# A tau-thresholded attention with a gated FFN on one core: plain float32 scores on halves of the rows in place of split ones, k kept for two chunks, 70 crossbar tiles and a new order

## The chip, the cores and the metric

The kernel runs on one core of one Trainium2 chip. The metric is the device time in microseconds; the kernel before takes 888.61 us, the median of three runs (888.23 to 890.14). One further run was profiled.

## What is computed

Eight batches of 576 tokens pass through an attention with eight heads of 64 channels and then through an FFN with a gate made by a three-tap convolution over the tokens:

```
scores = scale * q @ k.T                       # 576 x 576 per batch and head, float32
thresh = max(scores, axis=-1) - tau
scores = where(scores >= thresh, scores, -1e9)
attn = softmax(scores)                         # with 1e-9 added to the sum
x = concat over heads of attn @ v              # 576 x 512 per batch
h = relu(x @ w_in)                             # 512 -> 1024
conv = sum over 3 taps of conv_w[k] * shifted h
out = (h * sigmoid(conv)) @ w_out              # 1024 -> 512
```

## The kernel before

**Tiling.** Heads are taken in pairs, four pairs to a batch. The tokens of a batch are 4 full tiles of 128 rows and one of 64; tiles 0 and 1 are one chunk, tiles 2, 3 and 4 the next, so there are 16 chunks, 64 pairs of heads in chunks, and 160 units (one tile of one pair of heads). A full tile has two heads of scores, each 128 x 576 in two PSUM banks of 288 columns; the small tile has both heads in one buffer. That makes 288 score buffers in all, held in two PSUM buffers (`ps_s`).

**A unit** (`unit`, L573). TensorE makes the scores, VectorE takes the row maximum (L612), ScalarE the exponential (L619), VectorE masks it and sums (L622), and GpSimd (or ScalarE, L658) scales the result `em` by the reciprocal of the sum (L660).

**Turning `em`.** The product with v needs `em` with keys on the partitions, in the buffer `eT`. Most tiles are turned on TensorE: nine 128 x 128 transposes to a full tile (`transposes`, L719), gathered four at a time in a PSUM buffer `ps_t` and moved out by ScalarE (L714). The others go over the DMA crossbar (`cross`, L675): `em` is copied as two planes of 16-bit halves into `parts`, one plane by ScalarE (L337) and one by GpSimd (L339), `parts` is written to DRAM as `rows` (L692), and two transposing DMAs read it back into `eT` (L697). The table `CROSS` says how many full tiles of a chunk and pair go that way: 42 in all, none in batch 0.

**Product and FFN.** `attend` (L762) multiplies `eT` by v: first `mixed` (L774), 64-row matmuls on 64-column quarters of the array, then L783, 128 rows by 64 columns. The FFN (`mm1`, L799, and `mm2`, L854) uses the whole array with values rounded to fp32r and their remainders, three matmuls to a product. The FFN of a chunk is spread over the units of the chunk after it.

**Scores before.** In batch 0, and for every small tile, a score is a plain float32 product (L597): the 64 channels lie twice on the 128 partitions, the first half of the array makes keys 0 to 287 and the second half keys 288 to 575 at the same time. For the full tiles of batches 1 to 7 `split` is set (L604): q and k are each cut into a part rounded to fp32r and the remainder, these are stacked on the 128 partitions, and a head takes four fp32r matmuls of the whole array. `prep_k` (L532) and `prep_q` (L546) make these parts: two activations and a subtraction for k (L537, L538, L344), one activation and a subtraction for q (L552, L344), and DMAs that copy the parts to the other half of the partitions (L526, L560).

**The order.** Nothing runs in the order in which it is written. Every step is recorded with an engine, a duration, a rank and what it reads and writes; `Plan.run` then plays them through with a clock of its own and emits the instructions in the order that results. The rank is lowered by the entry of `AHEAD` for the kind of step. TensorE's steps have a kind: `full` (whole array), `turn` (transpose), `rows` and `cols` (parts of the array). The table `SWITCH` holds what a change of kind costs in this clock, and `KEEP` how much rank it may give up to avoid one. Each engine then executes its own list in order and waits on semaphores.

Of the kernel before, what the change touches and what calls it, by code (L numbers as in the profile page):

```python
# [22 lines left out]
AHEAD = {'mask': -0.546, 'norm': 0.0, 'parts': 0.747, 'gate': 0.0, 'evac': 0.244, 'low': 0.0, 's': 8.8, 's4': 7.75, 't': 2.623, 'a': 4.072, 'prep': 5.282, 'w': 2.013, 'load': 10.996}  # L23

LATENCY = {'pe': 159.52, 'act': 151.014, 'dve': 99.075, 'pool': 67.058, 'ring': 1611.881}

HOLD = {'pool': 162.449, 'dve': 91.329}
# [3 lines left out]
NEAR = 16  # L31
# [3 lines left out]
MOE = (2, 2)  # L35
BACKLOG = {'pool': 6860.0, 'dve': 120.0, 'act': 9000000000.0}
WRATE = (1.704, 1.59)
# [18 lines left out]
CROSS = ((1, 0, 1, 0), (1, 1, 1, 1))  # L56
LATE = {'load': 663.0, 'copy': 382.0, 'rows': 456.0, 'turn': 383.0}

KEEP = {'rows': 3.209, 'cols': 1.6, 'turn': 3.226, 'full': 1.708}
# [18 lines left out]


class Later:  # L80


    def __init__(self, view, n):
        self.view, self.shape = view, (n,)

    def __getitem__(self, key):
        return self.view()[key]
# [169 lines left out]
def tile_tau_attention_gated_ffn(  # L257
# [3 lines left out]
    qt: bass.AP,  # L261
    kt: bass.AP,
# [102 lines left out]
    def split(src, n, name, high, low, hr, lr, queue="sp"):  # L365
# [3 lines left out]
        stage = plan.buf(wk, "ks", 4, [P, 2, S], U32, name)  # L369
        value = plan.buf(wk, "xq", 2, [P, 2, 2 * P], U32, f"{name}_f")  # L370

        def flat():
            return stage[:].rearrange("p a b -> p (a b)")[:, :2 * n]
# [5 lines left out]
        def v(dtype=F32):  # L379
            return value[:].rearrange("p a b -> p (a b)")[:, :n].bitcast(dtype)  # L380
# [51 lines left out]
    QW = 2 * P  # L432
# [62 lines left out]
    def plain(b):  # L495
        return b == 0

    def prep_rows(i, b, p, o, w, tag):

        k = plan.buf(wk, "xk", 2, [P, S + D], F32, f"k_{i}")  # L500
        q = plan.buf(wk, tag, 2, [P, 2, w], F32, f"{tag}_{i}")
        a = AHEAD["prep"]

        if i:
            put(S + D, lambda: nc.sync.dma_start(k[:], kp[b, p]), w=[(k, 0), (k, 1)], ahead=a + 2)
# [6 lines left out]
        if w < P:  # L512
            op("act", act(2 * w), lambda: nc.scalar.activation(q[:], q[:], AF.Copy, scale=0.125), w=[(q, 0), (q, 1)], ahead=a)
            return k, q
        for j in range(2):
            op("act", act(w), lambda j=j: nc.scalar.activation(q[:, j], q[:, j], AF.Copy, scale=0.125), w=[(q, j)], ahead=a)
        return k, q

    def halves(dst, src, of, ahead):

# [384 lines left out]
    def prep(i, j):  # L905
        if i >= len(pairs):
            return
# [124 lines left out]
```

## Time and profile before

| | |
|---|---|
| median of three runs | 888.61 us (888.23 to 890.14) |
| profiled execution | 891.74 us |
| its span, first to last instruction | 889.9 us |
| granted TensorE clock, mean | 0.998 |

The span is 1.8 us shorter than the profiled execution's own time, and that execution is 3.1 us longer than the median. In the profile PE is TensorE's matmuls and PEld its weight loads, DVE is VectorE, ACT ScalarE, POOL GpSimd and SP the queue that issues most DMAs. A float32 matmul stands in the profile as two matmul instructions, each of which streams all columns; an fp32r one stands as one. In a timeline row the first number is the start and the second the length until the last of the merged instructions has ended; since matmuls are pipelined, the time that one takes from the next is read from start to start.

### The profile page before, as it was taken

The numbers are of one execution on the slowest core, as the hardware profiler recorded it, in microseconds if no ns is written. First come the engines' busy times: TensorE is split into PE (matmuls) and PEld (weight loads), VectorE is DVE, ScalarE is ACT, GpSimd is POOL, SyncE is SP. The second block draws the span as 40 slices with busy tenths as digits, with TensorE's granted clock in tenths as the row PEclk, the third lists the DMA queues.
The fourth block names the chain that finished last, engine by engine and source line by source line (L and its number), as shares of the span: only waits on it lengthen the run. The fifth ranks groups of instructions, "written<-read, shape, count | busy, mean of one in ns | idle before, by whom it ended". The sixth has DMA issues, their size and how long they took to land.

```text
span 889.9 us, 18227 instructions
## 1 busy us (share of the span) xinstructions
PE 861.2 (97%) x5930; PEld 691.7 (78%) x5930; DVE 748.0 (84%) x1902; ACT 712.5 (80%) x1489; POOL 476.8 (54%) x617
## 2 busy tenths in 40 slices
PE   4899999999999999999999999999999999999998
PEld 2445778778778788878888788897888888887896
DVE  5999999988989689987979689996998879997542
ACT  5989898888878787888877788887877888885642
POOL 3465865646646555565645556564663655553322
PEclk9999999999999999999999999999999999999999
DMA  7554366588855777659754697548955578454200
GB/s 235 177 166 140 92 178 163 142 223 205 222 147 136 207 187 202 144 157 239 194 170 115 155 238 197 141 118 242 225 150 131 156 219 211 117 150 106 66 24 36
DMA packets 176702, 145.22 MB, mean 163 GB/s; under 512 B 115552, under 2 KB 146528, under 8 KB 176608
## 3 DMA queue, kind: packets, MB, share of 16 engines
q1 hardware_dynamic: 175744, 142.15, 60.3%
q10 hardware_dynamic: 864, 1.90, 0.6%
q8 instruction: 48, 0.79, 0.4%
q14 instruction: 46, 0.38, 0.1%
HBM read 50.62 MB, written 34.21 MB: 95 GB/s over the span
## 4 chain that ended last, share of the span: by engine, by line
PE 80%; ACT 9%; DVE 6%; DMA 3%; issue 2%; SPq 0%; POOL 0%; ACTq 0%; DVEq 0%
PE po L863 20%; PE ph L812 19%; PE ps_s L604 13%; PE pa L783 12%; PE ps_t L719 9%; PE ps_s L597 4%; DVE em L622 2%; ACT eT L714 2%; ACT em L619 2%; PE pa L774 2%; DVE few L612 2%; DMA xk<-in_kt_dram 1%; PE pw_stage L418 1%; DMA k<-in_kp_dram 1%; DMA ks<-xk 1%
## 5 line engine op out<-in xcount | busy, mean ns | idle before, releaser
L660 POOL TENSOR_SCALAR em<-em,few 128x576 f32<-128x576 f32 x231 | 190.7, 832 | 185.9 <-DVE few L646 151.3
L612 DVE TENSOR_REDUCE few<-ps_s 128x1 f32<-128x576 f32 x288 | 210.7, 748 | 37.4 <-PE ps_s L597 20.0
L619 ACT ACTIVATE em<-ps_s,few 128x576 f32<-128x576 f32 x288 | 206.1, 739 | 43.0 <-DVE few L612 40.4
L812 PE MATMUL ph<-x,w1h 128*128 128x322 f32 (+1 forms) x1024 | 238.4, 304 | 0.5 <-ACT hp L821 0.5
L622 DVE SCALAR_TENSOR_TENSOR em<-ps_s,few,em 128x576 f32<-128x576 f32 x288 | 225.3, 811 | 14.6 <-ACT em L619 8.5
L344 POOL TENSOR_TENSOR gl<-t,gh 128x255 fp32r<-128x255 f32 (+9 forms) x192 | 123.4, 652 | 163.7 <-ACT gh L842 157.8
L812 PEld LDWEIGHTS ph<-x,w1h 128*128 128x128 f32 x1024 | 174.0, 189 | 2.1 <-issue 1.1
L714 ACT ACTIVATE eT<-ps_t 128x512 f32<-128x512 f32 (+2 forms) x332 | 149.1, 474 | 10.6 <-PE ps_t L719 8.4
L604 PE MATMUL ps_s<-ks,qs 128*128 128x288 f32 x896 | 151.9, 304 | 2.6 <-DVE em L622 0.6
L812 PE MATMUL ph<-x,w1l 128*128 128x322 f32 (+1 forms) x512 | 151.2, 295 | 0.0
L604 PEld LDWEIGHTS ps_s<-ks,qs 128*128 128x128 f32 x896 | 127.5, 188 | 27.5 <-issue 19.7
L719 PE MATMUL ps_t<-ident,em 128*128 128x128 f32 x934 | 137.0, 277 | 5.1 <-ACT eT L714 3.3
L783 PE MATMUL pa<-eT,v 128*64 128x320 f32 (+1 forms) x1024 | 132.8, 410 | 0.0
L719 PEld LDWEIGHTS ps_t<-ident,em 128*128 128x128 f32 x934 | 109.1, 142 | 27.5 <-issue 8.0
L863 PE MATMUL po<-w2h,gh 128*128 128x512 f32 x288 | 117.5, 408 | 0.0
L783 PEld LDWEIGHTS pa<-eT,v 128*64 128x64 f32 x1024 | 70.1, 137 | 58.2 <-issue 15.4
L863 PE MATMUL po<-w2l,gh 128*128 128x512 f32 x288 | 112.9, 392 | 0.0
L863 PE MATMUL po<-w2h,gl 128*128 128x512 f32 x288 | 112.9, 392 | 0.0
L827 DVE SCALAR_TENSOR_TENSOR t<-hp,cr 128x321 f32<-128x321 f32 (+1 forms) x128 | 82.4, 645 | 22.7 <-ACT hp L821 21.3
L812 PEld LDWEIGHTS ph<-x,w1l 128*128 128x128 f32 x512 | 96.7, 189 | 0.3
L832 DVE SCALAR_TENSOR_TENSOR t<-t,hp 128x321 f32<-128x321 f32 (+1 forms) x128 | 76.7, 600 | 12.6 <-ACT t L834 12.0
L827 DVE SCALAR_TENSOR_TENSOR t<-hp,cr,t 128x321 f32<-128x321 f32 (+1 forms) x128 | 85.7, 672 | 0.5
(78 smaller groups left out, 1079.1 us busy)
## 6 DMA issues: line engine op xcount, KB each, us to landing
rows<-parts SPq DMA_DIRECT2D x42, 576.0 KB, 3.4
qs<-qs SPq DMA_DIRECT2D x168, 128.0 KB, 2.9
k<-in_kp_dram SPq DMA_DIRECT2D x35, 320.0 KB, 3.4
v<-in_vc_dram SPq DMA_DIRECT2D x36, 288.0 KB, 4.2
out_dram<-ot SPq DMA_DIRECT2D x36, 256.0 KB, 2.6
xk<-in_kt_dram SPq DMA_DIRECT2D x28, 288.0 KB, 3.7
ks<-xk SPq DMA_DIRECT2D x56, 144.0 KB, 3.6
xq<-in_qt_dram SPq DMA_DIRECT2D x56, 128.0 KB, 3.0
```

The source lines that it names most:

```text
L344: engines[e].tensor_tensor(dst, x, y, op=ALU.subtract)
L604: nc.tensor.matmul(ps[:, c, :CH], lhsT=q[:, i, h, o:o + n], rhs=k[:, h, c * CH:(c + 1) * CH], start=(i == 0), stop=(i == 1))
L612: nc.vector.tensor_reduce(few[:rows, nm], ps[:rows, :, :CH], op=ALU.max, axis=mybir.AxisListType.XY, negate=True)
L619: nc.scalar.activation(view(), ps[:rows, :, :CH], AF.Exp, bias=few[:rows, nm])
L622: nc.vector.scalar_tensor_tensor(view(), ps[:rows, :, :CH], few[:rows, th], view(), op0=ALU.is_ge, op1=ALU.mult, accum_out=few[:rows, total])
L660: engines[e].tensor_scalar(sl, sl, LEAST, few[:rows, 10 + h:11 + h], op0=ALU.add, op1=ALU.mult)
L714: "act", act(w, True), lambda dst=dst, src=src: nc.scalar.activation(dst(), src(pt), AF.Copy),
L719: nc.tensor.transpose(out=pt[:, at:at + P], in_=em[:, int(b * P):int(b * P) + P], identity=ident[:])
L783: nc.tensor.matmul(pa[j * D:(j + 1) * D, :w], lhsT=vt[:, blk, :], rhs=eT[:, :w // D, blk, :], start=False, stop=(r == 3))
L812: nc.tensor.matmul(ph[:, :an], lhsT=w1[w][:, cb, fs], rhs=xs[cb][:, h, :an], start=(cb == 0 and i == 0), stop=(cb == NCB - 1 and i == 2))
L827: nc.vector.scalar_tensor_tensor(t[:, :kn], hp[:, o + k:o + kn + k], cr[:, j, f:f + 1], y, op0=ALU.mult, op1=ALU.add)
L863: nc.tensor.matmul(po[:], lhsT=x[:, f, at:at + P], rhs=w[:, f, :], start=(f == 0 and i == 0), stop=(f == NFB - 1 and i == 2))
```

## The change

All scores become plain float32 products on halves of the rows, as batch 0 had them. `split`, `prep_k`, `prep_q` and `halves` go, with the inputs `qt` and `kt` in which q and k lay once. For every pair of heads `prep` now loads q doubled over the partitions, and k doubled in the first chunk of a batch; k stays in its buffer for the second chunk (`KEEPK`, six buffers). The factor 0.125 is applied to k once (`eighth`), where batch 0 applied it to q in each chunk. `CROSS` sends 70 full tiles over the crossbar instead of 42: one tile of every pair in the even chunks, and two or one in the odd ones. The weights get staging buffers of their own. The numbers that steer `Plan.run` are replaced (`AHEAD`, `LATENCY`, `HOLD`, `KEEP`, `LATE`, `MOE`, `NEAR`, `WRATE`); of these a few lines are shown, since what they do is seen in the order only.

```diff
-NEAR = 16
+NEAR = 8
...
-MOE = (2, 2)
+MOE = (2, 3)
...
-WRATE = (1.704, 1.59)
+WRATE = (1.767, 1.972)
...
-CROSS = ((1, 0, 1, 0), (1, 1, 1, 1))
+KEEPK = 1
+XKB = 6
+CROSS = ((1, 1, 1, 1), (2, 1, 2, 1))
...
+        k = whole[i - NP][0] if o and KEEPK else plan.buf(wk, "xk", XKB, [P, S + D], F32, f"k_{i}")
+        q = plan.buf(wk, "q", QB, [P, 2, w], F32, f"q_{i}")
...
+                def eighth(e, x=x):
+                    copy(e, x(), x(), 0.125)
+
+                op("act", act(n), eighth, w=parts, ahead=a, other=[("pool", pool1(n)), ("dve", 65 + n * 0.53)] if i else [], port=True)
...
-                for c in range(2):
-                    for i in range(2):
+                for r, j in enumerate(js):
+                    for c in range(2):
+                        on = slice(c * D, (c + 1) * D)
+                        at = j * CH + r * D
                         nc.tensor.matmul(
-                            ps[:, c, :CH], lhsT=q[:, i, h, o:o + n], rhs=k[:, h, c * CH:(c + 1) * CH], start=(i == 0), stop=(i == 1)
+                            ps[r * n:(r + 1) * n, c, :CH], lhsT=q[on, j, o:o + n], rhs=k[on, at:at + CH],
+                            start=True, stop=True
                         )
...
-                "pe", 534 if split else 490, mm, w=[(ps, 0)],
+                "pe", 490, mm, w=[(ps, 0)],
```

What this does to the lists of the engines: on PE the 224 groups of split scores (four matmuls each) become 224 groups of plain ones, and 322 groups of transposes become 238 (934 transposes become 682). The rows here and in the prediction name tiles as the program does: `ps_s` scores, `pa` the product with v, `ph` and `po` the first and second product of the FFN, `ps_t` transposes.

The first place is PE in batch 3, at the scores of pair 1 in the first chunk (`ps_s_0` and `ps_s_1` are the two heads of a tile; the chunk has two tiles). Before:

```order
L604 MATMUL ps_s_0_3991<-ks_1_3743,qs_3804 128x288 x4
L774 MATMUL pa_4000<-eT_3762,v_2822 64x320 x2
L774 MATMUL pa_4003<-eT_3855,v_2862 64x320 x2
L604 MATMUL ps_s_1_4013<-ks_1_3743,qs_3804 128x288 x4
L783 MATMUL pa_4000<-eT_3762,v_2822 64x320 x8
L783 MATMUL pa_4003<-eT_3855,v_2862 64x320 x8
L604 MATMUL ps_s_0_4071<-ks_1_3743,qs_3804 128x288 x4
L604 MATMUL ps_s_1_4079<-ks_1_3743,qs_3804 128x288 x4
L812 MATMUL ph_4_4088<-x_3055,w1h 128x256
```

and now:

```order
L549 MATMUL ps_s_0_3598<-k_2302,q_3445 128x288 x2
L549 MATMUL ps_s_1_3606<-k_2302,q_3445 128x288 x2
L720 MATMUL pa_3613<-eT_3361,v_2615 64x320 x2
L720 MATMUL pa_3616<-eT_3454,v_2623 64x320 x2
L729 MATMUL pa_3613<-eT_3361,v_2615 64x320 x8
L729 MATMUL pa_3616<-eT_3454,v_2623 64x320 x8
L549 MATMUL ps_s_0_3662<-k_2302,q_3445 128x288 x2
L549 MATMUL ps_s_1_3670<-k_2302,q_3445 128x288 x2
L665 MATMUL ps_t_0_3674<-ident,em_3543 128x128 x4
L758 MATMUL ph_5_3682<-x_2698,w1h 128x256
```

The two heads of a tile now stand together and beside the products with v, where one head stood between two of these products before.

The second place is PE a little later in the same batch, where scores stand in the middle of the second product of the FFN. Before:

```order
L863 MATMUL po_4235<-w2h,gl 128x512
L863 MATMUL po_4235<-w2l,gh 128x512
L604 MATMUL ps_s_0_4256<-ks_2_4055,qs_4008 128x288 x4
L604 MATMUL ps_s_1_4264<-ks_2_4055,qs_4008 128x288 x4
L863 MATMUL po_4235<-w2h,gh 128x512
```

and now, at the first product of the FFN:

```order
L758 MATMUL ph_6_3715<-x_2973,w1h 128x256
L549 MATMUL ps_s_0_3739<-k_2926,q_3548 128x288 x2
L549 MATMUL ps_s_1_3747<-k_2926,q_3548 128x288 x2
L758 MATMUL ph_7_3752<-x_2698,w1h 128x256
L758 MATMUL ph_7_3752<-x_2698,w1l 128x256
```

Here the scores still stand alone between two stretches of the FFN, but they now use the array in halves, while the FFN on both sides uses the whole of it.

The third place is the SP queue in the same batch. Before:

```order
L526 DMA ks_0_3728<-xk_0_3653 64x576
L697 DMA_TRANSPOSE eT_3762<-rows_3609 128x9x128 x2
L692 DMA rows_3806<-parts_3770 128x2304
L526 DMA ks_0_3728<-xk_0_3653 64x576
L570 DMA v_3821<-in_vc_dram 128x576
L526 DMA ks_1_3743<-xk_1_3671 64x576 x2
L560 DMA qs_3804<-qs_3804 64x2x256 x2
L697 DMA_TRANSPOSE eT_3855<-rows_3806 128x9x128 x2
```

and now:

```order
L500 DMA k_3322<-in_kp_dram 128x640
L638 DMA rows_3338<-parts_3324 128x2304
L643 DMA_TRANSPOSE eT_3361<-rows_3278 128x9x128 x2
L643 DMA_TRANSPOSE eT_3361<-rows_3338 128x9x128 x2
L523 DMA v_3418<-in_vc_dram 128x576
L523 DMA v_3423<-in_vc_dram 128x576
L638 DMA rows_3430<-parts_3415 128x2304
```

The copies between the halves of the partitions are gone from the queue, and two crossbar tiles of one pair (`rows_3278` and `rows_3338`, both into `eT_3361`) now follow each other.

More of the change, by code (lines that the diff above doesn't have):

```diff
@@ L55 @@
 EMS = 5
[L56 to L59 removed]
+KEEPK = 1
+XKB = 6
+STB = 3
+ETB = 2
+PTB = 1
+QB = 2
+CROSS = ((1, 1, 1, 1), (2, 1, 2, 1))
+LATE = {'load': 663.0, 'copy': 114.0, 'rows': -19.0, 'turn': 737.0}
+KEEP = {'rows': 3.449, 'cols': 2.129, 'turn': 2.26, 'full': 1.604}
 class Buf:
@@ L511, in prep_rows @@
                 put(w, lambda j=j: nc.sync.dma_start(q[:, j], qd[b, p, :, j, o:o + w]), w=[(q, j)], ahead=210 - 10 * j)
[L512 to L519, printed above, removed]
-        x, view, parts = src
-        for part, head in of:
-            j, half = part
-            n = view.shape[-1]
-            put(
-                n, lambda j=j, half=half, head=head: nc.sync.dma_start(
-                    dst[half * D:(half + 1) * D, j, :n].bitcast(F32), view[head * D:(head + 1) * D].bitcast(F32)
-                ), issue=560, rows=D, late=LATE["copy"],
-                w=[(dst, part)], r=[(x, parts[head])], ahead=ahead
-            )
@@ L546, in prep_q @@
[L546 to L564 removed]
+        if not (o and KEEPK):
+            cuts = [(S + D, lambda: k[:], [(k, 0), (k, 1)])] if i else [
+                (on.stop - on.start, lambda on=on: k[:, on], [(k, j)]) for j, on in enumerate((slice(0, CH), slice(CH, S + D)))
+            ]
+            for n, x, parts in cuts:
+                def eighth(e, x=x):
+                    copy(e, x(), x(), 0.125)
+                op("act", act(n), eighth, w=parts, ahead=a, other=[("pool", pool1(n)), ("dve", 65 + n * 0.53)] if i else [], port=True)
@@ L627, in unit @@
             op(
-                "pe", 534 if split else 490, mm, w=[(ps, 0)],
-                r=[(k, (h, i)) for i in range(2)] + [(q, (x, h, i)) for x in range(2) for i in range(2)] if split else [(x, j) for x in (k, q) for j in js], ahead=a, kind="full" if split else "rows"
+                "pe", 490, mm, w=[(ps, 0)],
+                r=[(x, j) for x in (k, q) for j in js], ahead=a, kind="rows"
             )
@@ L672, in crossed @@
         c, p = pairs[i]
-        return not plain(chunks[c].b) and t in [x for x in order(i) if TILES[x][1] == P][:CROSS[c % 2][p]]
+        return chunks[c].b > 0 and t in [x for x in order(i) if TILES[x][1] == P][:CROSS[c % 2][p]]
     def cross(u, em, eT, off):
-        parts = plan.buf(wk, "parts", 1, [P, 2, 2 * S], U16, f"parts_{u}")
+        parts = plan.buf(wk, "parts", PTB, [P, 2, 2 * S], U16, f"parts_{u}")
         rows = plan.buf(far, "rows", FAR, [2 * P, 2 * S], U16, f"rows_{u}")
@@ L960, in tile_tau_attention_gated_ffn @@
                     waiting = []
-            for j in range(2):
-                if t == tiles[min(j, len(tiles) - 1)]:
-                    prep(i + 1, j)
+            if t == tiles[0]:
+                prep(i + 1)
             if t == tiles[-1] and p == NP - 1:
```

113 lines of the change are left out of this document (22 added, 91 removed).

## The prediction

> **What bounds the kernel now.** I read the table of stretches first, then the waits, then TensorE's timeline from start to start.
>
> ```profile
> PE 861.2 (97%) x5930; PEld 691.7 (78%) x5930; DVE 748.0 (84%) x1902; ACT 712.5 (80%) x1489; POOL 476.8 (54%) x617
> ```
>
> The stretches give, in order, the busy time of PE, PEld, DVE, ACT and POOL, with the number of instructions, then the granted clock, the share of the DMA engines and GB/s.
>
> ```profile
> 0.00:100.00 100.00, 80.28 (x477) 47.26 (x479) 83.24 (x210) 82.37 (x165) 53.92 (x70) 0.98 0.52 167
> 400.00:500.00 100.00, 99.70 (x700) 84.50 (x697) 85.50 (x220) 82.61 (x175) 57.66 (x74) 1.00 0.68 176
> 800.00:890.00 90.00, 85.97 (x532) 71.48 (x530) 44.95 (x101) 45.03 (x103) 26.53 (x37) 1.00 0.20 59
> ```
>
> PE is idle for 20 us in the first 100, for 4 in the last 90, and hardly at all in between (0.3 us in the middle row). No other engine is above 86% there. So after the start the time is what PE's list costs, and a microsecond of it counts as one. What PE still waits for:
>
> ```profile
> PEld ps_t L719 <- ACT eT L714: 5.8, 15, 1.1
> PEld ps_t L719 <- POOL em L660: 3.5, 6, 1.6
> PEld ps_s L597 <- DVE em L622: 3.3, 6, 1.3
> ```
>
> These are weight loads, where such waits show even if the matmul before is still counted as busy: 9.3 us belong to transposes, to their PSUM buffer being emptied and to `em` being scaled. All three are small.
>
> **The change on PE: transposes.** Eight transposes in the middle of the FFN's second product:
>
> ```profile
> 304.09 1.04 PE L719 MATMUL ps_t<-ident,em 128*128 128x128 f32 x8
> 304.88 0.48 PE L863 MATMUL po<-w2h,gh 128*128 128x512 f32 x1
> 305.20 0.39 PE L863 MATMUL po<-w2h,gl 128*128 128x512 f32 x1
> 305.43 0.40 PE L863 MATMUL po<-w2l,gh 128*128 128x512 f32 x1
> ```
>
> From start to start they take 0.79 us, and the matmul behind them 0.32 where the next takes 0.23, so 0.88 us in all, 0.11 each. Twenty-eight more tiles leave PE with nine transposes each: 252 x 0.11 = 27.7 us less.
>
> **Scores.** Split ones, two heads:
>
> ```profile
> 382.69 0.39 PE L863 MATMUL po<-w2l,gh 128*128 128x512 f32 x1
> 382.91 1.21 PE L604 MATMUL ps_s<-ks,qs 128*128 128x288 f32 x8
> 383.96 0.39 PE L863 MATMUL po<-w2h,gh 128*128 128x512 f32 x1
> ```
>
> 1.05 us for two heads, 0.525 each, and nothing is lost on either side. Plain ones exist in batch 0, first one head and then two:
>
> ```profile
> 102.14 0.28 PE L812 MATMUL ph<-x,w1l 128*128 128x256 f32 x1
> 102.26 0.28 PE L812 MATMUL ph<-x,w1h 128*128 128x256 f32 x1
> 102.47 0.76 PE L597 MATMUL ps_s<-k,qs 64*128 64x288 f32 x4
> 103.15 1.09 PE L719 MATMUL ps_t<-ident,em 128*128 128x128 f32 x8
> 108.24 1.24 PE L597 MATMUL ps_s<-k,qs 64*128 64x288 f32 x8
> 109.41 0.76 PE L774 MATMUL pa<-eT,v 64*64 64x320 f32 x4
> ```
>
> One head takes 0.68 us and two take 1.17, so a head inside such a stretch costs 0.49 and a stretch carries 0.2 us besides. 224 heads x (0.525 - 0.485) = 9 us less.
>
> **Changes of the array's shape.** The 0.2 us are not all. The L812 ahead of the scores takes 0.21 us until they start, where the one before took 0.12: 0.09 to enter. On the way out to the whole array, here behind the scores of a small tile:
>
> ```profile
> 172.09 1.20 PE L597 MATMUL ps_s<-k,q 64*64 64x288 f32 x16
> 173.22 0.50 PE L863 MATMUL po<-w2h,gh 128*128 128x512 f32 x1
> 173.56 0.40 PE L863 MATMUL po<-w2h,gl 128*128 128x512 f32 x1
> 173.80 0.39 PE L863 MATMUL po<-w2l,gh 128*128 128x512 f32 x1
> ```
>
> The first L863 behind a stretch of halves takes 0.34 where the next takes 0.24, another 0.10. So a stretch between FFN matmuls loses 0.09 + 0.20 + 0.10 = 0.39 us in two changes of shape, and one that leads to transposes some 0.35: 0.17 to 0.20 for a change. It costs as much inside such a stretch, between shapes that are both parts of the array:
>
> ```profile
> 49.78 0.76 PE L597 MATMUL ps_s<-k,qs 64*128 64x288 f32 x4
> 50.47 0.65 PE L774 MATMUL pa<-eT,v 64*64 64x256 f32 x4
> 51.05 0.76 PE L597 MATMUL ps_s<-k,qs 64*128 64x288 f32 x4
> ```
>
> Here too the head takes 0.69. Counted through PE's list by the shape of each row (whole array with transposes, 64 x 64, 64 x 128, 128 x 64), there are 162 changes before and 371 now. The stretches in parts of the array go from 63 to 142; the rest of the increase lies inside them, where scores now stand beside the products. 209 x 0.18 = 37.6 us more; with 0.15, which leaves out the slow first pass of the smaller shapes, 31, and with 0.20, 42.
>
> [...] If only the ends of stretches counted, 79 more stretches x 0.36 = 28 us would make PE's sum -8.7 us in place of the one that follows.
>
> PE's sum: -27.7 - 9.0 + 37.6 = +0.9 us (-5 to +5). What the transposes save, the changes of shape take back.
>
> **The other engines.** They matter only through PE's waits. Of ACT's rows the change touches:
>
> ```profile
> L714 ACT ACTIVATE eT<-ps_t 128x512 f32<-128x512 f32 x204 | 116.9, 600 | 7.5 <-PE ps_t L719 6.4
> L337 ACT ACTIVATE parts<-em 128x1152 uint16<-128x1152 uint16 x42 | 49.0, 1168 | 0.8 <-POOL em L660 0.4
> L552 ACT ACTIVATE qs<-xq 128x256 fp32r<-128x256 f32 x56 | 23.4, 418 | 15.9 <-PE ps_s L604 15.0 <-DMA qs<-qs 0.6
> L538 ACT ACTIVATE ks<-xk 128x576 fp32r<-128x576 f32 x28 | 19.1, 683 | 0.2
> L537 ACT ACTIVATE xk<-xk 128x576 f32<-128x576 f32 x28 | 19.0, 679 | 1.8 <-DMA xk<-in_kt_dram 1.7
> ```
>
> Less: 56 evictions x 0.600 = 33.6, and 23.4 + 19.1 + 19.0. More: 28 x 1.168 = 32.7 for `parts`, and 33 scalings of 640 elements, estimated at 0.683 x 640 / 576 = 0.76 us each, 25. ACT ends some 37 us lower. POOL loses its 84 subtractions and gains 28 copies; DVE's list is the same but for three short instructions. So the engines that empty the transposes' buffers have more room, and there are 27% fewer transposes: of the 9.3 us of waits I take off 2.5 for their number and 1.5 for ACT, 4 us. From below: all 9.3 us and some of the idle start, 10 less. From above: new waits of 10 us, about what the transposes wait for now, since a two-head stretch needs both score buffers free at once.
>
> The start stays DVE's and ACT's (83 and 82 us busy of 100): batch 0 keeps its scores and transposes, k is scaled once instead of q twice, and the first FFN product stands behind 26 score buffers instead of 28. I cost it at nothing, and at 3 us either way if that cover fails. The kept k saves loads that SP issues far ahead.
>
> **The crossbar.** Each of the 28 tiles brings one write and two transposing DMAs to SP, in whose queue the 252 copies of parts (168 of q, 84 of k) are gone.
>
> ```profile
> L697 SPq DMA_TRANSPOSE eT<-rows x84: 1278/1475/2714, 133.7 to 829.0; - x84
> L692 SPq DMA_DIRECT2D rows<-parts x42: 332/372/1154, 128.3 to 824.8; - x42
> rows<-parts SPq DMA_DIRECT2D x42, 576.0 KB, 3.4
> eT<-rows SPq DMA_TRANSPOSE x84, 4.0
> ```
>
> 140 transposes x 1.475 = 207 us of SP's 890, against 124: not a bound, but every load behind one waits 3 us for a pair. What a tile needs from its scores to `eT`:
>
> ```profile
> L622 DVE SCALAR_TENSOR_TENSOR em<-ps_s,few,em 128x576 f32<-128x576 f32 x288 | 225.3, 811 | 14.6 <-ACT em L619 8.5
> L612 DVE TENSOR_REDUCE few<-ps_s 128x1 f32<-128x576 f32 x288 | 210.7, 748 | 37.4 <-PE ps_s L597 20.0
> L619 ACT ACTIVATE em<-ps_s,few 128x576 f32<-128x576 f32 x288 | 206.1, 739 | 43.0 <-DVE few L612 40.4
> L660 POOL TENSOR_SCALAR em<-em,few 128x576 f32<-128x576 f32 x231 | 190.7, 832 | 185.9 <-DVE few L646 151.3
> ```
>
> Two maxima, an exponential, two masks, two scalings, a copy, the write, one issue and the last landing: 1.5 + 0.74 + 1.62 + 1.66 + 1.17 + 3.4 + 1.48 + 4.0 = 15.6 us with nothing in the way. In the order, with the durations above, the shortest way from such a tile's scores to the product that needs it is 18 us of PE's work before and after; 6 tiles lie under 21 us before and 10 now. No wait of the products for these DMAs shows in the table before, so I cost it at nothing.
>
> [...]
>
> **The sum.** +0.9 - 4 = -3.1 us. On the profiled execution, 891.74 us, that is 888.6; it was 3.1 us above the median, and the same difference on the median, 888.6, gives 885.5 us.
>
> **Rivals.**
> *No difference.* PE's waits stay as they are: +0.9 us, 889.5. For it: PE is at 99.7% in the middle, and what ACT saves was hardly waited for.
> *Slower: the crossbar's tile comes late.* Place: the product of two pairs, which waits for all of their tiles; there are 28 such products after batch 0. If the queues on the way (SP behind another pair of transposes, 3 us; the one `parts` buffer, read for 3.4 us by the tile before) add 3 us to the 15.6, the tightest tiles pass 18 us and PE stands still. At half a microsecond for each product that is 14 us: 888.6 + 14 + 1 = 903.6. For it: two tiles of one pair now follow each other. Against it: the copies that stood between are gone.
> *Slower: changes of shape at 0.20 us and new waits for both score buffers at once.* +5 + 5 = 10 us, 898.6: a wait of 0.05 us at each of some 100 stretches of scores decides it.
> *A larger gain.* Changes of shape at 0.15 and waits down by 9: -5 - 9 = 874.6. For it: part of a change may fall into time that PE would have waited anyway.
> *The scores do not run in pairs* as they do in batch 0, because loads of the FFN stand next to them. The row at 172.09, plain scores next to FFN matmuls in batch 1, speaks against it: 1.13 us for two buffers; I give it nothing.
>
> **Chances.** About 0.2%, 1.8 us, is what a measurement of this kernel can tell from no change, so faster ends at 886.8 and slower begins at 890.4. Forecast 0.40, no difference 0.22, late crossbar 0.17, dearer changes 0.11, larger gain 0.10. That makes faster 0.50, same 0.22, slower 0.28. The late crossbar costs anything from nothing to 14 us and more, by how late the tiles are. The range goes from the larger gain, 874, to the dearer changes, 899, and leaves out the dearest part of the late crossbar, about 1 in 10, and as much below. The forecast's own range is 876 to 887.
>
> **What would show it.** In the changed profile PE should have 682 transposes, no split scores, and L549 in groups of 0.49 us a head plus 0.2 at each stretch; the first FFN matmul behind a stretch should take 0.10 us more. In the middle PE should stay above 98% busy. ACT should come to about 675 us. Waits of L729 or L720 for `eT<-rows` would mean the late crossbar; many waits of L549 for DVE's L568 the buffers. I am wrong if PE's busy share falls under 95% in the middle stretches, or if a change of shape costs clearly other than 0.15 to 0.20 us.

## The result, and the profile after

The changed kernel takes 883.16 us, the median of four runs (881.94 to 884.28). The kernel before, run beside it, takes 888.82 us (888.23 to 890.14). The ratio is 0.9934 [0.9916, 0.9952], so it is faster by 5.9 us with an interval from 4.3 to 7.5. The forecast was 885.5 us, and its own range went from 876 to 887. The profiled execution of the changed kernel took 883.45 us with a span of 881.7 us, 8.2 us less than the span before.

The engines' busy time over the whole span, from the page of the changed kernel:

```profile
PE 851.9 (97%) x5678; PEld 617.5 (70%) x5678; DVE 724.6 (82%) x1905; ACT 670.9 (76%) x1327; POOL 422.2 (48%) x558
```

Its stretches, in the columns that the prediction explains:

```profile
0.00:100.00 100.00, 76.29 (x455) 44.89 (x455) 77.27 (x204) 79.27 (x150) 49.36 (x66) 0.98 0.51 161
400.00:500.00 100.00, 99.89 (x676) 74.69 (x674) 83.63 (x220) 77.29 (x153) 47.86 (x65) 1.00 0.64 167
800.00:882.00 82.00, 77.56 (x478) 63.25 (x477) 39.23 (x88) 39.58 (x88) 24.38 (x33) 1.00 0.24 70
```

The kernel is still bound as before. PE is full in the middle, and the other engines are lower. The first 100 us got worse, as the waits below show; PE is busy for 76.29 us there, where it was 80.28.

**The scores.** The timeline of PE in the changed kernel, where a stretch with one head of scores stands in the first product of the FFN:

```profile
410.48 0.28 PE L758 MATMUL ph<-x,w1l 128*128 128x256 f32 x1
410.60 0.28 PE L758 MATMUL ph<-x,w1h 128*128 128x256 f32 x1
410.81 0.76 PE L549 MATMUL ps_s<-k,q 64*128 64x288 f32 x4
411.50 0.38 PE L758 MATMUL ph<-x,w1h 128*128 128x256 f32 x1
411.72 0.28 PE L758 MATMUL ph<-x,w1l 128*128 128x256 f32 x1
411.83 0.28 PE L758 MATMUL ph<-x,w1h 128*128 128x256 f32 x1
```

Read from start to start. The L758 ahead of the scores takes 0.21 us where the one before it took 0.12. The head takes 0.69 and the first L758 behind it 0.22 where the next takes 0.11. That is 0.09 + 0.20 + 0.11 beside 0.49 for the head: 0.40 us for two changes of the array's shape. A split head, which uses the whole array as the FFN does, had none there: the L863 ahead of the two at 382.91 in the prediction's rows takes 0.22 us and the one behind them 0.23 (the next starts at 384.19), the price of an L863 among its own.

**PE's time, in three parts.** I added up PE's list in the same way over the whole trace. Each matmul's time is the distance from its start to the next start. "Work" is what its kind takes inside a stretch of its own kind (a transpose 0.109 us, a plain head 0.486, a split head 0.532, an FFN matmul 0.118, 0.150 or 0.227 by its columns, and so on). "Shape" is what its changes of shape cost by such rows (0.09 to 0.10 to leave a shape, 0.05 to 0.11 for the slow first pass in the new one). "Wait" is what is left. It holds the waits that the table of waits shows, waits of weight loads behind a matmul that is still counted as busy, time at a lower granted clock (down to 0.50, as the rows of split70 in the last section show), and errors of the prices. A difference of 2 or 3 us in it says little. Work and shape are thus counts times prices that were read in these traces; only the sum is timed.

| kernel | work | shape | wait | sum, first to last matmul |
|---|---|---|---|---|
| before | 807.2 | 28.4 | 41.5 | 877.2 |
| after | 769.4 | 67.1 | 31.7 | 868.3 |
| difference | -37.8 | +38.7 | -9.8 | -8.9 |

The span fell by 8.2 and not by 8.9, mostly since the first matmul starts at 9.31 us where it started at 8.73. Of the wait, 21.5 us lay in the first 120 us before and 25.2 lie there now. Behind them it fell from 20.0 to 6.5. These parts come from one profiled execution of each kernel. The one before was 3.1 us above its median and the one after 0.3, so up to 2.8 of the 9.8 us may belong to the execution and not to the kernel.

What PE waited for in the first 120 us, of the kernel before:

```profile
PE ps_s L597 <- ACT qs L516: 8.7, 1, 8.7
PE ps_s L597 <- DVE em L622: 7.8, 10, 2.1
```

and of the changed one:

```profile
PE ps_s L549 <- ACT k L331: 11.3, 2, 9.3
PE ps_s L549 <- DVE em L568: 4.9, 5, 2.1
PE ps_t L665 <- ACT eT L660: 3.5, 3, 1.6
PE ps_t L665 <- POOL em L606: 2.8, 1, 2.8
```

The first matmul now waits for k to be scaled, 9.3 us, and a second wait for k of 2 us follows. The middle of the program in one row, before and then after:

```profile
120.00:800.00 680.00, 675.42 (x4791) 558.15 (x4790) 601.75 (x1552) 567.39 (x1185) 382.20 (x496) 1.00 0.68 177
```

```profile
120.00:800.00 680.00, 678.59 (x4616) 496.57 (x4615) 588.97 (x1563) 534.05 (x1051) 337.91 (x448) 1.00 0.66 174
```

PE goes from 4.6 us idle to 1.4. The rest of the lower wait lies inside its busy time, where the table of waits does not show it, or in the errors of the prices.

### The profile page after: what moved, and what is told of

Same layout as the page of the kernel before. It is cut to its first block, busy times and chain, and to the rows that moved or that the text cites. A ratio compares the mean times of both kernels' runs of the same rounds, so it can differ in the third digit from the quotient of the medians.

```text
span 881.7 us, 17007 instructions
## 1 busy us (share of the span) xinstructions
PE 851.9 (97%) x5678; PEld 617.5 (70%) x5678; DVE 724.6 (82%) x1905; ACT 670.9 (76%) x1327; POOL 422.2 (48%) x558
## 3 DMA queue, kind: packets, MB, share of 16 engines
q1 hardware_dynamic: 210112, 138.54, 58.1%
## 4 chain that ended last, share of the span: by engine, by line
PE 91%; ACT 3%; DVE 3%; DMA 1%; issue 1%; SPq 0%; POOL 0%; ACTq 0%; DVEq 0%; POOLq 0%
PE ph L758 23%; PE po L809 23%; PE ps_s L549 19%; PE pa L729 14%; PE ps_t L665 9%; PE pa L720 2%; DVE few L558 1%; ACT em L565 1%; PE pw_stage L412 1%; DMA q<-in_qd_dram 1%; DVE em L568 1%; ACT eT L660 1%; DMA v<-in_vc_dram 0%; DVE stage_f L393 0%; ACT stage L387 0%
## 5 line engine op out<-in xcount | busy, mean ns | idle before, releaser
L606 POOL TENSOR_SCALAR em<-em,few 128x576 f32<-128x576 f32 x228 | 184.2, 815 | 185.4 <-DVE few L592 168.5
L565 ACT ACTIVATE em<-ps_s,few 128x576 f32<-128x576 f32 x288 | 208.7, 740 | 56.4 <-DVE few L558 54.7
L758 PE MATMUL ph<-x,w1h 128*128 128x322 f32 (+1 forms) x1024 | 231.8, 305 | 0.6 <-ACT hp L767 0.6
L549 PE MATMUL ps_s<-k,q 64*128 64x288 f32 (+1 forms) x1280 | 192.0, 439 | 17.6 <-ACT k L331 11.3
L758 PEld LDWEIGHTS ph<-x,w1h 128*128 128x128 f32 x1024 | 171.8, 190 | 16.1 <-issue 12.8
L549 PEld LDWEIGHTS ps_s<-k,q 64*128 64x128 f32 (+1 forms) x1280 | 94.1, 177 | 85.2 <-issue 44.4
L758 PE MATMUL ph<-x,w1l 128*128 128x322 f32 (+1 forms) x512 | 151.0, 295 | 0.0
L660 ACT ACTIVATE eT<-ps_t 64x64 f32<-64x64 f32 (+3 forms) x262 | 114.4, 452 | 16.3 <-PE ps_t L665 14.9
L665 PE MATMUL ps_t<-ident,em 128*128 128x128 f32 x682 | 104.4, 281 | 7.6 <-ACT eT L660 3.5
L729 PEld LDWEIGHTS pa<-eT,v 128*64 128x64 f32 x1024 | 70.4, 137 | 58.8 <-issue 15.3
L665 PEld LDWEIGHTS ps_t<-ident,em 128*128 128x128 f32 x682 | 77.0, 141 | 45.6 <-issue 22.0
L758 PEld LDWEIGHTS ph<-x,w1l 128*128 128x128 f32 x512 | 96.5, 189 | 0.2
L331 ACT ACTIVATE parts<-em 128x1152 uint16<-128x1152 uint16 x70 | 81.4, 1163 | 19.0 <-POOL em L606 18.6
L333 POOL COPY parts<-em 128x1152 uint16<-128x1152 uint16 x70 | 82.7, 1182 | 15.1 <-DMA rows<-parts 6.9
```

The lines of the kernel that those rows point to most:

```text
L333: engines[e].tensor_copy(dst, src)
L549: nc.tensor.matmul(ps[r * n:(r + 1) * n, c, :CH], lhsT=q[on, j, o:o + n], rhs=k[on, at:at + CH], start=True, stop=True)
L565: nc.scalar.activation(view(), ps[:rows, :, :CH], AF.Exp, bias=few[:rows, nm])
L606: engines[e].tensor_scalar(sl, sl, LEAST, few[:rows, 10 + h:11 + h], op0=ALU.add, op1=ALU.mult)
L660: "act", act(w, True), lambda dst=dst, src=src: nc.scalar.activation(dst(), src(pt), AF.Copy),
L665: nc.tensor.transpose(out=pt[:, at:at + P], in_=em[:, int(b * P):int(b * P) + P], identity=ident[:])
```

## The experiments

The theory behind them: PE's list sets the time, so a kernel's time follows from its list, and the other engines, the queues and the steering numbers add waits of a few microseconds. The rival: the list is a wash by the prediction's own sum, and what decides is the load on the queues and on the engines that feed PE, and how well the order fits it.

Each kernel was timed beside the kernel before, and ratios are to that. A difference from the changed kernel is the difference of the two ratios times 888.8 us, good to about 2 us. Three of the kernels (`plain70_extra_dma`, `plain70_extra_issues`, `plain70_busy_act`) add idle work that no result depends on. PE's parts of them all, as in the table above, are from one profiled execution each. It lay 4.4 us above the kernel's median in plain84, 2.8 above in plain70_extra_dma, and 1.3 to 2.2 below in plain42, split70, plain70_old_numbers and plain70_busy_act.

| kernel | ratio [95%] | from after, us | work | shape | wait |
|---|---|---|---|---|---|
| plain42 | 1.0209 [1.0192, 1.0226] | +24.4 | 796.9 | 65.6 | 29.3 |
| split70 | 1.0247 [1.0230, 1.0265] | +27.8 | 779.7 | 31.8 | 83.9 |
| split42_new_numbers | 1.0139 [1.0124, 1.0154] | +18.2 | 807.2 | 27.8 | 52.8 |
| plain70_old_numbers | 1.0106 [1.0087, 1.0125] | +15.3 | 769.4 | 71.0 | 40.8 |
| plain70_extra_dma | 1.0411 [1.0395, 1.0427] | +42.4 | 769.4 | 67.1 | 76.9 |
| plain70_extra_issues | 1.0233 [1.0219, 1.0247] | +26.6 | 769.4 | 67.1 | 58.1 |
| plain84 | 1.0177 [1.0156, 1.0198] | +21.6 | 755.7 | 70.7 | 65.8 |
| plain70_busy_act | 0.9959 [0.9947, 0.9972] | +2.2 | 769.4 | 67.1 | 32.8 |
| plain70_out_act_same | 0.9943 [0.9929, 0.9956] | +0.8 | 769.4 | 67.1 | 34.3 |
| plain70_switch | 1.0010 [1.0001, 1.0019] | +6.8 | 769.4 | 65.7 | 39.2 |
| plain70_old_clock | 1.0012 [1.0003, 1.0021] | +6.9 | 769.4 | 70.5 | 35.1 |
| plain70_old_ranks | 1.0127 [1.0113, 1.0142] | +17.2 | 769.4 | 73.5 | 43.5 |

One thing limits most of these comparisons. Wherever `CROSS` or a steering number is changed, the order is planned anew, under numbers that were not fitted to the result. plain70_switch shows what that alone can cost: 6.8 us with a list 1.4 us shorter. The two extra-DMA runs, plain70_busy_act and plain70_out_act_same keep the order of the changed kernel.

**plain42: the change without the 28 crossbar tiles.**

```diff
-CROSS = ((1, 1, 1, 1), (2, 1, 2, 1))
+CROSS = ((1, 0, 1, 0), (1, 1, 1, 1))
```

> The changed kernel with the old crossbar table: 42 tiles instead of 70, the rest as changed, order planned anew. PE's list then has 934 transposes again (252 more, 27.7 us at 0.11) and 366 changes of shape instead of 371 (1 us less). Theory (PE's list sets the time, microsecond for microsecond): 883.2 + 27 = 910 us, a few more if the waits on the transposes' buffers come back (up to 915). Rival (the transposes were hidden, and the gain comes from the lighter ACT and POOL): ACT and POOL stay light, so within 3 us of 883.

It took 908.00 us. PE's work is 27.5 us more than in the changed kernel, the price of 252 transposes at 0.11, and shape and wait are nearly the same. That is the theory's time. So the plain scores alone, with the new numbers, do not pay: it is the transposes taken off PE that do, and here the 28 tiles come nearly free.

**split70: the kernel before with the 28 crossbar tiles.**

```diff
-CROSS = ((1, 0, 1, 0), (1, 1, 1, 1))
+CROSS = ((1, 1, 1, 1), (2, 1, 2, 1))
```

> The kernel before with nothing but the new crossbar table: split scores, 70 tiles. PE's list loses 252 transposes (27.7 us) and gains 22 changes of shape (184 instead of 162, 4 us): 24 us less. Theory: 888.8 - 24 = 865 us if nothing else becomes the bound, and then faster than both kernels; 875 if half of it goes into waits, since ACT keeps the preparation of q and k and about 33 us of copies come to it and to POOL for 38 us of evictions that ACT loses. Rival (ACT, POOL and the DMAs pay for it: the tiles come late or the copies queue): 885 to 895, with waits of the products for eT<-rows or of PE for em.

It took 911.60 us, and here the theory fell; the time is above the rival's 895 too. PE's list shrank as expected, by 24 us, and the time rose by 22: the wait doubled. Two stretches of it:

```profile
200.00:300.00 100.00, 96.86 (x651) 76.61 (x650) 89.99 (x236) 82.72 (x167) 62.85 (x78) 1.00 0.93 225
600.00:700.00 100.00, 92.52 (x618) 74.91 (x616) 83.39 (x205) 78.63 (x162) 52.99 (x69) 0.97 0.89 218
```

The DMA share is 0.93 and 0.89, where the stretch of the kernel before that the prediction shows had 0.68. The groups of DMAs of split70:

```profile
rows<-parts SPq DMA_DIRECT2D x70, 576.0 KB, 3.8
qs<-qs SPq DMA_DIRECT2D x168, 128.0 KB, 3.2
```

The write of `rows` lands in 3.8 us, where it took 3.4 before, and SP issues 168 copies of q beside it. But PE's waits hold 1 us for a copy of q and nothing for `eT<-rows`. The longest of its waits in the middle is this (timeline of PE in split70):

```profile
539.95 0.39 PE L863 MATMUL po<-w2l,gh 128*128 128x512 f32 x1
544.96 0.64 PE L812 MATMUL ph<-x,w1h 128*128 128x322 f32 x1 [4.63 <-ACT ot L870]
545.40 0.47 PE L812 MATMUL ph<-x,w1l 128*128 128x322 f32 x1
```

ACT runs through this time without a gap, with two exponentials, both steps of k's preparation, a copy to `parts` and a scaling, before it comes to the eviction of `ot` for which PE waits. So this wait shows at ACT, which is late with its list, and not at a DMA. That the load on the DMAs made ACT late is not shown by these rows.

**split42_new_numbers: the kernel before with the new steering numbers.**

```diff
-NEAR = 16
+NEAR = 8
...
-MOE = (2, 2)
+MOE = (2, 3)
...
-WRATE = (1.704, 1.59)
+WRATE = (1.767, 1.972)
```

and `AHEAD`, `LATENCY`, `HOLD`, `LATE` and `KEEP` as in the changed kernel.

> The kernel before with the changed kernel's steering numbers (AHEAD, LATENCY, HOLD, NEAR, MOE, WRATE, LATE, KEEP) and nothing else: split scores, 42 tiles. PE's list is the same sum (160 changes of shape against 162). Theory: the numbers alone move little, 886 to 891. Rival (the new order is what brought the waits down): 880 to 884, with as few waits of PE in the middle as the changed kernel has.

It took 901.95 us, outside both expectations. PE's list is the same to 0.6 us, and the wait is 11.3 us more. The numbers that belong to the changed kernel hurt the old one, so they do not lower waits by themselves.

**plain70_old_numbers: the changed kernel with the old steering numbers.**

```diff
-NEAR = 8
+NEAR = 16
...
-MOE = (2, 3)
+MOE = (2, 2)
...
-WRATE = (1.767, 1.972)
+WRATE = (1.704, 1.59)
```

and the other five tables as before.

> The changed kernel with the steering numbers of the kernel before, the rest as changed. PE's list has 384 changes of shape instead of 371 (3.9 us at up to 0.2 us and slower first passes, so the list is 3.9 us longer). Theory: 883.2 + 4 = 887, with 1 or 2 us of waits on top, up to 889. Rival (the new order is what brought the gain): 889 or more, PE waiting in the middle as before the change.

It took 898.05 us, 15.3 more than the changed kernel: 3.9 in shape and 9.1 in wait in the profiled runs. That is the rival's side. The longest wait of PE itself between 120 and 800 us is one for a score buffer:

```profile
PE ps_s L549 <- DVE em L568: 4.2, 5, 1.5
```

where the changed kernel has only

```profile
PE ps_s L549 <- issue: 1.1, 2, 0.6
```

Without the new numbers the whole change would have been slower than the kernel before, by 9.4 us. The four runs so far also compare plain scores (with the kept k and the copies dropped) with split ones at equal numbers. With 70 tiles and the old numbers, plain scores are 12.5 us faster (1.0106 against 1.0247): work -10.3, shape +39.2, wait -43.1. With 42 tiles and the new numbers, they are 6.2 us slower (1.0209 against 1.0139): work -10.3, shape +37.8, wait -23.5. What the plain scores lose in changes of shape they win back mostly in waits. They win more with 70 tiles and the old numbers than with 42 and the new ones; since both differ, these runs do not say which of the two makes it so.

**plain70_extra_dma and plain70_extra_issues: what the dropped copies of q and k may have cost.** The changed kernel with 252 more DMAs in SP's queue, as many as there were copies of parts, three behind a load of q and three more where k is loaded too. They go from DRAM to DRAM, and nothing waits for them. PE's, ACT's, DVE's and POOL's lists are those of the changed kernel. Once they move 128 or 144 KB each, like the copies, and once 4 KB.

```diff
+            def load_q():
+                nc.sync.dma_start(q[:], qd[b, p, :, :, o:o + w])
+                if b:
+                    for j in range(3):
...
+                        nc.sync.dma_start(spare[:, :, :256], qd[b, p, 0:64, :, 0:256])
```

```diff
-                        nc.sync.dma_start(spare[:, :, :256], qd[b, p, 0:64, :, 0:256])
+                        nc.sync.dma_start(spare[:, :, :8], qd[b, p, 0:64, :, 0:8])
```

> The changed kernel with 252 DMAs added that nobody waits for, as many and as large as the copies between partition halves that the change removed (three of 128 KB with each load of q, three of 144 KB with each load of k, after batch 0, from DRAM to a spare DRAM buffer). The lists of PE, ACT, DVE and POOL stay as they are. Split scores with 70 tiles had a PE list shorter by 24 us than the kernel before and yet took 22 us longer, with the DMA engines at 75% of the span (83 to 93% in the middle) against 60. Theory: the room on the DMAs pays for the tiles; without it, loads and crossbar tiles come late: 895 to 925 us here, with the DMA share in the middle above 0.8 and PE waiting for what DMAs bring. Rival (in the split kernel it was the longer way of q and k over ACT, POOL and a copy, not the load on the DMAs): within 4 us of 883.

> The same 252 added DMAs, but of 4 KB each (64 rows, 16 floats a row): SP issues as many as before the change, the DMA engines move next to nothing more. If the place in SP's queue is what counts (252 issues of some 0.5 us, with every transpose and load behind them), it takes nearly what the full-sized copies take, 893 or more. If the DMA engines' time is what counts: within 4 us of 883.

The large ones took 925.43 us and the small ones 909.54: 42.4 and 26.6 us more than the changed kernel, with the same lists on every computing engine. The large ones lie at the upper end of what was expected, and the small ones, though well above 893, take only part of the loss. So 26.6 us come with DMAs that carry next to nothing, and 15.8 more with the bytes. The small ones raise the share of the DMA engines between 120 and 800 us from 0.66 to only 0.69. So most of the 26.6 is likely the place in the queue, but not all of it need be: the crossbar's write lands later there too, in 3.8 us. In the large case the crossbar's write (3.1 us to landing in the changed kernel) and the spare copies read:

```profile
rows<-parts SPq DMA_DIRECT2D x70, 576.0 KB, 4.4
spare_q<-in_qd_dram SPq DMA_DIRECT2D x168, 128.0 KB, 3.7
```

In the small case the copies hold the queue for this long (min, median, max in ns):

```profile
L506 SPq DMA_DIRECT2D spare_q<-in_qd_dram x168: 512/597/2056, 101.3 to 815.5; - x168
```

and ACT then waits for k, from 120 to 800 us:

```profile
ACT k L331 <- DMA k<-in_kp_dram: 34.1, 17, 3.9
```

where the changed kernel has, in the same stretch,

```profile
ACT k L331 <- DMA k<-in_kp_dram: 0.2, 1, 0.2
```

These waits are 2 us long on average. Each stops ACT in its list, and with it the evictions and exponentials behind it. That PE's wait grew by 26.4 us in this way is argued; it was not followed wait by wait. These 252 stand in clumps of three or six, where the old copies were spread out, so the 42 us are not the price of the old copies. They show that the cover of the queue is thin.

**plain84: still more crossbar.**

```diff
-CROSS = ((1, 1, 1, 1), (2, 1, 2, 1))
+CROSS = ((1, 1, 1, 1), (2, 2, 2, 2))
```

> The changed kernel with 84 crossbar tiles (both full tiles of every pair in the odd chunks), the rest as changed, order planned anew. PE's list loses 126 transposes (13.9 us) and gains 15 changes of shape (3.6 us): 10 us less. The DMA share goes from 58% to some 65 or 66 (28 more tiles made it 15 points in the split kernel). Theory: 883 - 10 = 873 if the waits stay, as the DMAs have room to about the three quarters where the split kernel was late; up to 882 if the waits grow as they did with other steering numbers. Rival (the crossbar is already at its limit): 885 or more, with waits of the products for eT<-rows.

It took 903.17 us, on the rival's side, but no wait of PE for `eT<-rows` shows. PE's list is 10 us shorter and its wait 34 longer, in an execution 4.4 us above the median. One of the waits that grew is POOL's for the one `parts` buffer, here in plain84:

```profile
POOL parts L333 <- DMA rows<-parts: 15.5, 11, 2.6
```

and in the changed kernel:

```profile
POOL parts L333 <- DMA rows<-parts: 6.9, 6, 2.8
```

That row explains 9 us of POOL's time and not all of PE's 34. The steering numbers are those of 70 tiles, which may do the rest; that was not separated.

**plain70_busy_act: ACT's relief taken back.** The changed kernel with 140 copies of 0.30 us on ACT, one at the first head of each unit from unit 20 on, 42 us in all; the other lists are the same.

```diff
-            def exp(ps=ps, nm=nm, view=view):
+            def exp(ps=ps, nm=nm, view=view, h=h):
+                if h == 0 and u >= 20:
+                    nc.scalar.activation(spare[:], ident[:], AF.Copy)
```

> The changed kernel with 140 idle copies on ACT (128 x 128 into a buffer that nobody reads, one ahead of the first exponential of each unit after batch 0), unknown to the planner: every other engine's list stays as it is. At 0.29 us each, the row of that shape before the change, ACT gets 40 us back, about what the change took from it (712.5 us before, 670.9 after). Theory of the prediction (ACT's room is part of what lowered PE's waits, 1.5 us of it): 884 to 888. Rival (PE sets the time and ACT's room is worth nothing): within 1.5 us of 883. Other rival (the exponentials stand in the chain that frees the score buffers, and each copy delays one): 140 x 0.05 to 0.1 us, 890 to 897.

It took 886.39 us, 2.2 more, hardly beyond the 2 us that such a difference is good to. ACT's busy time rose from 670.9 to 694.4 us:

```profile
PE 851.7 (97%) x5678; PEld 615.8 (70%) x5678; DVE 725.2 (82%) x1905; ACT 694.4 (79%) x1467; POOL 424.2 (48%) x558
```

That is 23.5 us and not 42, in good part since the records of neighbouring instructions on ACT overlap: in the changed kernel the exponential at 401.74 lasts 0.74 us and the next record starts at 402.38, 0.10 before its end, and 140 times that would be 14 of the 18.5 us. So only a good half of the 41.6 us by which the change had lowered ACT's busy time was taken back. The prediction's 1.5 us for ACT's room fits this, and so do nothing and twice as much; the run does not tell them apart.

**plain70_out_act_same: the stores out of SP's queue.** SP waits long for ACT ahead of each store of the output. Here ACT issues the store right behind its eviction.

```diff
-        op("act", act(DO, True), lambda: nc.scalar.activation(ot[:, :DO], po[:], AF.Copy), w=[(ot, 0)], r=[(po, 0)])
-        put(DO, lambda: nc.sync.dma_start(tokens[m * P:(m + 1) * P, :], ot[:, :DO]), r=[(ot, 0)])
+        def evict():
+            nc.scalar.activation(ot[:, :DO], po[:], AF.Copy)
+            nc.scalar.dma_start(tokens[m * P:(m + 1) * P, :], ot[:, :DO])
```

> The changed kernel with the 36 output DMAs issued by ACT right behind the copy that fills their buffer, in place of SP; the lists of PE, DVE and POOL stay as they are. In the changed kernel SP stands 82.7 us in 23 waits for that copy, with every load and crossbar DMA behind it. Theory (what SP does late becomes waits of PE; 252 issues more cost 26 us): the waits of PE in the middle are only 6 us in 680, so at most that can be won, less 36 issues on ACT: 878 to 883. Rival (SP's stands are slack that the planner has counted on): 883 to 886.

It took 884.77 us, no difference from the changed kernel, as the rival had it. In the changed kernel these waits of SP are:

```profile
SPq L817 <- ACT ot L816: 82.7, 23, 21.5
```

With the stores gone, SP waits 198 us for ACT's half of `parts`, where it waited 160. So 38 of the 82.7 us that were won in the queue went into the next wait, and the time stayed: these waits were slack, unless the 36 issues on ACT ate a small gain (SP's issues of these stores took 0.34 us each, by the median, in the changed kernel). Here a queue that waited was not yet a queue that was late.

**plain70_switch: the planner told what a change of shape costs.** The table `SWITCH` set to the prices measured in the trace.

```diff
-    "rows": {"cols": 155, "turn": 160, "full": 208}, "cols": {"rows": 155, "turn": 155, "full": 205},
-    "turn": {"rows": 145, "cols": 145, "full": 5}, "full": {"rows": 145, "cols": 145, "turn": 0},
+    "rows": {"cols": 150, "turn": 155, "full": 205}, "cols": {"rows": 205, "turn": 155, "full": 205},
+    "turn": {"rows": 200, "cols": 145, "full": 5}, "full": {"rows": 200, "cols": 145, "turn": 0},
```

> The changed kernel with the planner's table of what a change of shape costs set to what the traces show (0.200 us into scores of full tiles instead of 0.145, 0.205 from the products to scores instead of 0.155). Nothing else; the order then has 362 changes of shape instead of 371, and PE's list is 1.4 us shorter. Theory: 881 to 885, the steering numbers' effect on the waits (up to 10 us either way between sets so far) is the larger part. If the sign of the waits follows from how true the planner's clock is, it should fall below 883; if not, it may be 885 to 893.

It took 889.71 us, 6.8 more than the changed kernel and outside the theory's 881 to 885. The list came out 1.4 us shorter, and the wait 7.5 longer. A truer price in the planner did not make a better order. The likely reason, which was not tested, is that the other numbers were fitted to the old one.

**plain70_old_clock and plain70_old_ranks: which of the steering numbers matter.** The changed kernel with the old values of four numbers each: those that say when data is there, with `KEEP`, and those that say which step goes first. (`NEAR` is among the latter; it sets the unit from which ACT takes a share of the scalings.)

```diff
-LATE = {'load': 663.0, 'copy': 114.0, 'rows': -19.0, 'turn': 737.0}
+LATE = {'load': 663.0, 'copy': 382.0, 'rows': 456.0, 'turn': 383.0}
```

and `LATENCY`, `HOLD` and `KEEP` likewise in the one; in the other

```diff
-MOE = (2, 3)
+MOE = (2, 2)
```

and `AHEAD`, `NEAR` and `WRATE` likewise.

> The changed kernel with four of the old steering numbers (LATENCY, HOLD, LATE, KEEP: when the planner takes data to be there) and the other four (AHEAD, NEAR, MOE, WRATE: which step goes first) new. All eight old made 898. TensorE's list has 387 changes of array shape in place of 371, 3.4 us more. Theory (the numbers were fitted together, and each group carries about its own share of the list and of the waits): 888 to 893, waits of TensorE up by 2 to 6 us. Rival (these four alone carry the waits, since they tell the planner how late a transfer lands): 895 or more. Rival (the order is worth only its list): 886.5.

> The changed kernel with the other four old steering numbers (AHEAD, NEAR, MOE, WRATE: which step goes first), the numbers on when data is there new. 395 changes of array shape in TensorE's list, 6.4 us more than in the changed kernel. Theory (each group carries its own share): 890 to 895. Rival (these four carry nearly all of the 15 us that the old numbers cost): 897 or more. Rival (the order is worth only its list): 889.5.

They took 890.70 and 900.91 us. The first cost 6.9 us, 3.4 in shape and 3.4 in wait, as the theory had it. The second cost 17.2, within the error as much as all eight numbers together (15.3), so there the rival was right: the ranks carry most of the effect. And the two groups do not add up: 6.9 and 17.2 make 24, not 15.

## Why the prediction was right

**PE's list: right, term by term.** Predicted -27.7 (transposes) - 9.0 (scores) = -36.7 of work; -37.8 when the changed trace is priced. Predicted +37.6 for 209 more changes of shape; +38.7 in the traces, that is 0.185 us each. The sum, +0.9, came out at +0.9. The prices stood up too: a head inside its stretch costs 0.486 us where 0.485 was said. The term most in doubt was the changes inside a stretch. Two heads in the changed kernel, first behind FFN matmuls and then behind products with v:

```profile
406.96 0.39 PE L809 MATMUL po<-w2l,gh 128*128 128x512 f32 x1
407.28 1.24 PE L549 MATMUL ps_s<-k,q 64*128 64x288 f32 x8
408.45 0.66 PE L665 MATMUL ps_t<-ident,em 128*128 128x128 f32 x4
```

```profile
422.52 4.53 PE L729 MATMUL pa<-eT,v 128*64 128x320 f32 x32
426.98 1.24 PE L549 MATMUL ps_s<-k,q 64*128 64x288 f32 x8
428.15 0.66 PE L665 MATMUL ps_t<-ident,em 128*128 128x128 f32 x4
```

They take 1.17 us in both places, so a change into this shape costs the same inside a stretch, from another part of the array, as at its end, from the whole. With changes counted at the ends of stretches alone the sum would have been 9.6 us lower, -8.7. That the whole list then fell by 8.9 is no support for that count: by these rows it is a coincidence.

**The waits: right in sign, mis-sized, and for another reason.** The step "I take off 2.5 for their number and 1.5 for ACT, 4 us" came out at -9.8 by the table, or some 7 without what the profiled executions may add. The start, costed at "nothing, and at 3 us either way", is +3.7 of this, and the rest of the program -13.5. The bound from below, -10, held the total only because the two offset each other. The step counted the 9.3 us that the table of waits puts to transposes, while PE's waits from start to start were 41.5. And fewer transposes and more room on ACT are not what lowered them: with the old numbers the changed kernel has both, and its wait is 40.8, about that of the kernel before, 41.5; with the new ones it is 31.7. So the lower wait came with steering numbers fitted to the new kernel. The prediction counted the changes of shape in the new order, but gave the order no term of its own for waits. That the total came close to 885.5 is in this part luck. plain70_busy_act allows the 1.5 us for ACT, and does not prove it.

**On the median** the step is 5.7 us and not 8.2, since the profiled execution before was 3.1 us above its median and the one after 0.3. The forecast carried that difference through, and 2.3 us are left between 885.5 and 883.2.

**The crossbar: right number, wrong reason.** "No wait of the products for these DMAs shows in the table before, so I cost it at nothing." The number was right: against plain42 the 28 tiles save 27.5 us of work and add 2.4 of wait. But the same sentence would have costed split70's and plain84's tiles at nothing, and split70 lost 22 us against the kernel it was made from (before), plain84 22 us against its own (after). An order under numbers that were not fitted to it may be a good part of both. In neither does PE wait for `eT<-rows`; its waits are for ACT, for score buffers and the like. The likely reason that the 28 tiles were free here is that the change took 252 DMAs, 84 subtractions and 112 activations out at the same time. For the DMAs the two runs that put 252 back show that such room is needed, with order and lists unchanged, though theirs stand in clumps as the old copies did not. For the work of ACT and POOL it is argued. The rival of a late crossbar named a real danger, since more tiles can cost time, but the wait that it named did not show. The landing also stayed short, as these rows of the changed kernel show (first the issue on SP, min, median and max in ns, then the landing in us):

```profile
L643 SPq DMA_TRANSPOSE eT<-rows x140: 1269/1472/3192, 128.5 to 820.9; - x140
rows<-parts SPq DMA_DIRECT2D x70, 576.0 KB, 3.1
eT<-rows SPq DMA_TRANSPOSE x140, 4.1
```

**The other marks.** ACT came to 670.9 us where about 675 was said: the prediction counted 56 evictions of 512 columns, and 14 of 256 columns went as well (22 before, 8 now). PE stayed at 99.8% in the middle, and the first FFN matmul behind a stretch takes 0.11 us more. The prediction's sign "PE's busy share falls under 95%" is a blunt one: plain70_old_numbers never does so in the middle and is slower than before.

**What stays open.** How much of split70's wait belongs to the DMAs, to ACT and to POOL was not separated, since the old copies could not be taken away without the split scores. It was also not tried to fit new steering numbers to split70 or plain84, so no run says that 70 tiles is the best number, only that it is the best of 42, 70 and 84 under these numbers. No experiment beat the changed kernel.

## What to carry to other kernels

Price an engine's list from start to start, changes of array shape included. Here each term came out within 1.1 us of its forecast. But a shorter list helped here only as far as the queues and engines that feed it kept up: split70's list was 24 us shorter than before, and its time 22 longer. Two halves of a change can each be slower than nothing and together be faster: here split scores with 70 tiles and plain scores with 42 both lost about 20 us, of which an order planned under numbers that do not fit may be a part. Where an order comes from fitted numbers, these belong to one kernel; a change that replaces them needs a term for waits of its own, and an experiment with the old numbers.

## What the runs showed of the hardware

**In split70 TensorE's clock fell to 0.50 during a stand of 4.63 us, and the loss was longer than the stand.** The stretches of split70 around the wait of 4.63 us shown above, in columns as before (the granted clock is the third number from the end):

```profile
540.00:542.00 2.00, 0.33 (x2) 0.00 (x0) 1.70 (x5) 1.97 (x5) 2.00 (x4) 1.00 1.13 230
542.00:544.00 2.00, 0.00 (x0) 0.00 (x0) 1.02 (x5) 2.00 (x4) 2.00 (x4) 0.59 0.80 219
544.00:546.00 2.00, 1.04 (x4) 1.04 (x5) 0.00 (x0) 1.48 (x3) 1.20 (x1) 0.50 0.97 314
546.00:548.00 2.00, 2.00 (x12) 0.84 (x10) 0.00 (x0) 0.00 (x0) 0.00 (x0) 0.50 0.97 301
548.00:550.00 2.00, 2.00 (x14) 1.70 (x12) 0.57 (x1) 0.00 (x0) 0.00 (x0) 0.71 0.58 160
```

PE's last matmul ended at 540.34. Taken as 1.00 or 0.50 and nothing between, the means put the clock at 0.50 from about 542.4 to 549.2, 6.8 us, of which PE worked 4.2, from 544.96 on. The L812 at 545.40 takes 0.26 us from start to start, where the one at 556.50, at a clock of 1.00, takes 0.14. So by this estimate a wait that stands as 4.63 us in the table of waits cost another 2.1. Not every stand did this: after one of 2.8 us, at 18.5 us in the changed kernel, the clock stayed at 1.00. Over a whole span (1 - mean clock) x span is an upper estimate of the loss: 1.8 us in the kernel before and in the changed one (0.998), 10 in split70 (0.989), 20 in the profiled execution of plain70_extra_dma (0.978) and 10 to 12 in its others (0.987 to 0.989).

**252 small DMAs cost time in this queue.** At 4 KB each they hold SP for 0.6 us (0.597 x 252 = 150 us in all) and cost this kernel 26.6 us though nothing waits for them; with 32 times the bytes and more they cost 42.4.
